# Linear attention and a gated feed-forward layer: first-chunk projection in three float32r products, a new order of work, buffer slots by list, and 32 opening matmuls of ones

## Chip, cores and metric

One core of one Trainium2 chip. The metric is device time in microseconds (us) from one run of the program. The kernel before took 948.82 us (median of three runs, 946.91 to 949.45). All data is float32 in device memory.

## Reference

```python
# q, k, v: (8 batches, 8 heads, 576 positions, 64);  w_a, w_b: (512, 1536);  w_out: (1536, 512)
q_s = softmax(q, over the 64 channels)           # + 1e-9 in the denominator
k_s = softmax(k, over the 576 positions)
kv  = einsum('bhsd,bhse->bhde', k_s, v)
x   = einsum('bhsd,bhde->bhse', q_s, kv)         # -> (4608 tokens, 512)
out = ((x @ w_a) * (x @ w_b)) @ w_out            # -> (4608, 512)
```

## The kernel before, in words

**Chunks.** The 4608 tokens are worked in nine chunks of 512. A chunk needs its attention output x (four pieces of 128 channels by 512 tokens), the two wide products a and b (1536 columns each, in twelve blocks f of 128), their elementwise product g, and the projection of g with `w_out`, summed over the twelve f in four accumulators `po0` to `po3`, one for each 128 tokens.

**Precision.** Most products are made from two-part operands: a float32 value is rounded to float32r (high part, a ScalarE copy, line L202) and the rest is kept as a second float32r value (low part, a VectorE subtraction, L205). A product is then three float32r matmuls: high by high, high by low, low by high. The helper that makes both parts is `split`. `g_split` calls it for g, `split_wo` for a block of `w_out`.

**Chunks 1 to 8** run in six pairs of blocks each. A pair makes seven products in a Strassen manner (`product`, L685, 12 float32r matmuls of 256 columns each), combines them on VectorE and ScalarE into `cc`, splits g (`gh`, `gl`) and projects it (`project`, L706, 12 float32r matmuls of 512 columns for each f).

**Chunk 0** goes block by block, while weights, keys and queries are still coming in. `gate_part` (L660) makes a and b of block f with 24 float32r matmuls of 512 columns. `gate_half` copies a out of PSUM (ScalarE, L667) into a tile `ga` with the tag `gh0` or `gh1`, `gate_end` multiplies it by b (VectorE, L671), and `project_first` (L695) projects the result with plain float32 matmuls: four for each f, one for each 128 tokens. The plain form needs neither `g_split` nor `split_wo`; the splits of the twelve blocks of `w_out` are needed by chunk 1 first.

**Weights** arrive as 64-bit words and are turned into float32 by `float_parts`: two ScalarE passes (L226, L227), a VectorE shift (L230), a GpSimd addition (L233) and a VectorE join (L236). Steps `a.f`, `b.f` and `out.f` are this conversion for the blocks of `w_a`, `w_b` and `w_out`; from f = 4 on the converted block of `w_out` is moved by DMA into its lasting place (`wo_w<-wy`). `sums.i` makes sums of weight blocks on GpSimd for the seven products (L348), `w0.i` to `w6.i` fetch or make the operands, each into one of eight `ws` buffers.

**Order.** Every engine runs its instructions in the order in which they are issued. A table `ORDER` names, for each of five queues (PE is TensorE, DVE is VectorE, Activation is ScalarE, Pool is GpSimd, SP issues the DMAs), the steps in the order wanted: `gate.5*3` takes the next three instructions of that step, `gate.5:6` takes the one that is seventh among those left. What is not in the list comes behind it, in the order of a scheduler that works with the costs of a model. Before, the list of PE ends with the first pair of chunk 2 (`pair.6`).

**Buffers.** A tile pool hands out the buffers of one tag in turn (`ws` 8, `xo` 11, `wy` 8, and so on); a tile waits until the last reader of the tile that had its buffer before is done.

**Start.** The queries (`q_load`), keys (`k_load_t`) and values of chunk 0 come first. `mc`, `ek`: maximum and exponential of the keys; `qs`, `qe`: maximum and exponentials of the queries; `tr` (L969) and `pq` (L1027): transposes on TensorE; `pk`: key-value products (L437); `px` (L604): x; `xh`, `xl`: its two parts; `g00` and so on: `gate_part` of the first blocks.

Of the kernel before, what the change touches and what calls it, by code (L numbers as in the profile page):

```python
# [147 lines left out]
    ),  # L148
}


@with_exitstack
def linear_attention_then_gated_ffn(
# [18 lines left out]
    nc = tc.nc  # L172
# [1199 lines left out]
```

## Time and profile before

| what | value |
|---|---|
| runs, median of three | 948.82 us |
| profiled execution, own time | 951.55 us |
| its span, first to last instruction | 949.7 us |
| TensorE matmuls busy | 928.4 us, 98%, 6479 instructions |
| VectorE busy | 613.7 us, 65% |
| ScalarE busy | 390.5 us, 41% |
| GpSimd busy | 104.8 us, 11% |
| DMA | 282.64 MB, mean 298 GB/s |
| TensorE in the chain that ended last | 89% of the span |

The profiled execution is one run, 2.73 us above the median of the three; 1.85 us of its time lie outside the span. Busy time of TensorE is taken from modelled ends of pipelined matmuls, so the row cannot tell a TensorE at its peak from one that is held up for short times. A plain float32 matmul stands in the trace as two rows, so that the 48 of `project_first` are 96 rows.

### The profile page before, as it was taken

Reading aid. Unit: us, or ns where it says so; the run is one execution under the profiler, and the core shown is the slowest. Engines: PE = TensorE matmul, PEld = TensorE weight load, DVE = VectorE, ACT = ScalarE, POOL = GpSimd, SP = SyncE. Lnnn points to the kernel's source line nnn. Section 1 sums busy time; section 2 is a strip of 40 time slices with the busy share of each in tenths; the row PEclk is TensorE's granted clock in tenths of the full one; section 3 lists DMA queues with packets and bytes.
Section 4 is the critical chain, followed back from the end, with each engine's and each line's share of the span. In section 5 each row is a group of like instructions: output and inputs, shape, how many; then the busy total and the mean of one; then the engine's idle time right before and its main releaser. Section 6 shows DMA issues by size and latency. Waiting matters only on the chain.

```text
span 949.7 us, 17529 instructions
## 1 busy us (share of the span) xinstructions
PE 928.4 (98%) x6479; PEld 825.9 (87%) x6479; DVE 613.7 (65%) x1209; ACT 390.5 (41%) x1085; POOL 104.8 (11%) x88
## 2 busy tenths in 40 slices
PE   5999999999999999999999999999999999999998
PEld 4666668889899999999999999999999999999997
DVE  6978889788685656664757566665756456553443
ACT  7986856424362226222723153334422353121111
POOL 2544452330010001000100000000000000000000
PEclk9999999999999999999999999999999999999999
DMA  9999888899999869896989688976996789577761
GB/s 345 409 389 360 331 315 297 325 330 353 291 380 303 314 255 343 271 353 221 336 273 381 235 283 303 364 273 248 341 334 222 261 284 330 209 262 252 262 214 53
DMA packets 97588, 282.64 MB, mean 298 GB/s; under 512 B 11680, under 2 KB 12256, under 8 KB 97504
## 3 DMA queue, kind: packets, MB, share of 16 engines
q1 hardware_dynamic: 97504, 281.52, 82.7%
q8 instruction: 52, 0.85, 0.3%
q14 instruction: 32, 0.26, 0.1%
HBM read 241.40 MB, written 37.98 MB: 294 GB/s over the span
## 4 chain that ended last, share of the span: by engine, by line
PE 89%; DMA 4%; DVE 4%; SPq 1%; ACT 1%; issue 1%; DVEq 0%; ACTq 0%
PE po L706 27%; PE kp L685 13%; PE ka L685 13%; PE kx L685 13%; PE pt L660 7%; PE ky L685 7%; PE po L695 4%; PE px L616 2%; PE pk L437 2%; DMA ws<-dw 1%; DMA mr<-dq 1%; SPq L571 1%; DMA raw<-in_w_ab 1%; PE px L604 1%; DVE ws L205 1%
## 5 line engine op out<-in xcount | busy, mean ns | idle before, releaser
L706 PE MATMUL po<-wo_w,gh 128*128 128x512 f32 x768 | 227.3, 395 | 0.6 <-ACT gh L202 0.6
L685 PE MATMUL kx<-xo,ws 128*128 128x256 f32 x1152 | 163.1, 283 | 1.3 <-DMA ws<-dw 1.3
L685 PE MATMUL ka<-xo,ws 128*128 128x256 f32 x1152 | 160.8, 282 | 1.1 <-DVE cc L1313 1.1
L706 PEld LDWEIGHTS po<-wo_w,gh 128*128 128x128 f32 x768 | 138.1, 188 | 26.6 <-ACT gh L202 1.1
L685 PE MATMUL kp<-xo,ws 128*128 128x256 f32 x1152 | 158.2, 283 | 0.0
L685 PEld LDWEIGHTS ka<-xo,ws 128*128 128x128 f32 x1152 | 149.5, 188 | 5.5 <-DVE cc L1313 1.3
L685 PEld LDWEIGHTS kx<-xo,ws 128*128 128x128 f32 x1152 | 149.2, 188 | 5.4 <-issue 1.9
L685 PEld LDWEIGHTS kp<-xo,ws 128*128 128x128 f32 x1152 | 148.2, 188 | 4.8 <-issue 0.5
L706 PE MATMUL po<-wo_w,gl 128*128 128x512 f32 x384 | 137.3, 396 | 0.0
L202 ACT CAST gh<-cc 128x512 fp32r<-128x512 f32 x96 | 56.6, 621 | 142.4 <-DVE cc L1309 128.8
L1308 DVE TENSOR_TENSOR cc<-kp,u 128x512 f32<-128x512 f32 x48 | 33.1, 689 | 101.3 <-PE kp L685 101.1
L1296 ACT COPY cc<-kx 128x256 f32<-128x256 f32 x48 | 17.8, 372 | 168.5 <-PE kx L685 168.5
L660 PE MATMUL pt<-xo,ws 128*128 128x512 f32 x288 | 86.7, 441 | 0.0
L706 PEld LDWEIGHTS po<-wo_w,gl 128*128 128x128 f32 x384 | 71.2, 188 | 16.2 <-DVE gl L205 0.7
L530 ACT ACTIVATE qt<-qt,st 128x64 f32<-128x64 f32 x224 | 75.2, 340 | 21.3 <-DVE st L527 18.2
L1295 DVE TENSOR_TENSOR cc<-kp,u 128x512 f32<-128x512 f32 x48 | 33.1, 690 | 76.5 <-PE kp L685 76.2
L685 PE MATMUL ky<-xo,ws 128*128 128x256 f32 x576 | 77.0, 283 | 2.4 <-DMA ws<-dw 0.8
L660 PEld LDWEIGHTS pt<-xo,ws 128*128 128x128 f32 x288 | 53.5, 189 | 24.8 <-issue 13.8
L685 PEld LDWEIGHTS ky<-xo,ws 128*128 128x128 f32 x576 | 71.7, 188 | 3.5 <-DVE xf L802 2.1
L205 DVE TENSOR_TENSOR gl<-cc,gh 128x512 fp32r<-128x512 f32 x96 | 64.0, 685 | 10.7 <-ACT gh L202 10.6
L367 POOL PARTITION_ALL_REDUCE mx<-m x20 | 18.3, 916 | 446.0 <-DVE m L378 446.0
L1277 ACT COPY u<-kx 128x512 f32<-128x512 f32 x48 | 28.0, 584 | 93.8 <-PE kx L685 85.4
(147 smaller groups left out, 1145.1 us busy)
## 6 DMA issues: line engine op xcount, KB each, us to landing
ws<-dw SPq DMA_DIRECT2D x312, 512.0 KB, 5.3
dw<-ws SPq DMA_DIRECT2D x42, 512.0 KB, 6.4
mr<-dq SPq DMA_DIRECT2D x112, 128.0 KB, 4.3
raw<-in_w_ab SPq DMA_DIRECT2D x24, 512.0 KB, 8.3
out<-ot SPq DMA_DIRECT2D x36, 256.0 KB, 4.5
vt<-in_v SPq DMA_DIRECT2D x28, 325.0 KB, 7.1
qt<-in_q SPq DMA_DIRECT2D x32, 256.0 KB, 5.4
kt<-in_k SPq DMA_DIRECT2D x24, 320.0 KB, 5.2
```

The source lines that it names most:

```text
L202: nc.scalar.copy(out=hi, in_=src)
L205: return nc.vector.tensor_tensor(out=lo, in0=src, in1=hi.bitcast(F32), op=ALU.subtract)
L437: nc.tensor.matmul(pk[h * D:(h + 1) * D], kt[:, j, h], vt[:, j, h], start=(j == 0), stop=(j == J - 1),)
L530: nc.scalar.activation(out=qt[:, j, h], in_=qt[:, j, h], func=AF.Exp, bias=st[:, h, 0, j:j + 1], accum_out=st[:, h, 1, j:j + 1],)
L616: nc.tensor.matmul(px[:, s], w, m[:, s], start=(i == 0), stop=(i == 2))
L660: nc.tensor.matmul(pt, w[:, wp], x[g][:, xp], start=(g == 0 and i == 0), stop=(g == NP - 1 and i == 2),)
L685: ins = nc.tensor.matmul(pt[:, n], w[:, n, wp, c], x[:, xp, c], start=(first and n == 0 and i == 0), stop=(i == 5), skip_group_check=True,)
L695: nc.tensor.matmul(po[t], g[:, t * P:(t + 1) * P], wo_first[f], start=(f == 0), stop=(f == NF - 1),)
L706: ins = nc.tensor.matmul(po[t], a[:, ts], wo[f][:, w], start=(f == 0 and i == 0), stop=(f == NF - 1 and i == 2),)
L1277: nc.scalar.copy(out=u2, in_=kx)
L1295: nc.vector.tensor_tensor(out=cc[:, 3], in0=kp, in1=u3, op=ALU.add)
L1308: nc.vector.tensor_tensor(out=cc[:, 1], in0=kp, in1=u2, op=ALU.add)
```

## The change

It has five parts.

1. **Projection of chunk 0.** For f = 0, 1, 2 nothing changes (`PLAIN = 3`). For f = 3 to 11 `project_first` first splits g (`g_split`, one ScalarE copy and one VectorE subtraction) and then calls `project`, that is twelve float32r matmuls instead of four plain ones. `split_wo(f)` is called just ahead of it, no longer in the first pairs of chunk 1. For those f the tile `ga` is one of four parts of a tile with the tag `cc`, so that `gh` and `gl` are free for the two parts.
2. **32 matmuls of ones**, 128 by 128 in plain float32, into the accumulator bank `po3`, ahead of everything else on TensorE. Nobody reads the sums. The matrix of ones is set by GpSimd, as before.
3. **New order.** All five lists are new. The lists of PE and DVE reach to the end of chunk 2 (`pair.11`, `early.11`) instead of its first pair, SP's to the operands of `pair.11`. The first loads stand in the list too: the first queries come ahead of the first keys, and the identity matrix after them.
4. **Slots by list.** The pool is wrapped by a class that gives each tile a named slot with a buffer of its own: first by a list `SLOTS`, then the slot that was given longest ago.
5. **Attention in chunk 2** is no longer pinned behind the last VectorE combination of the pair; its place comes from the list.

```diff
     "PE": (
-        "tr1*4 tr0*5 tr1 pk0*10 pk1*10 pq0*4 tr2*5 pq1*4 px0 tr3:4 tr3*4 pq2*4 pk2*10 pk3*10 px1 "
-        "g00:6 g00:6 g00:6 g00*3 pq3*4 px2 g10:6 g10:6 g10:6 g10:6 g10:6 g10:6 g00*3 g10*3 g00*3 px3 "
...
+        "warm*32 tr0*5 tr1:4 pq0*4 tr1*4 pk0*10 pq1*4 pk1*8 px0 tr2:4 pk1*2 tr2*4 tr3*5 px1 pq3*4 "
+        "pk3*10 pk2*10 pq2*4 g00 g00:5 g00*2 g00:3*2 g00 g00:2 px2 g00 g10:6*2 g00:1 g10*2 g00:1 "
...
     "Activation": (
-        "ek0 qe0 qe0:5 qe0:1 ek1 qe0:3 qe1 qe0:1 qe0 cA1 qe0:1 qe0 cA0 ek2 wc00:1 wc00 qe2 qe2:3 "
...
+        "qe0 qe0:4 qe0:3 qe0 qe0:3 qe0:2 qe0:1 qe1 ek0 qe0 ek1 cA0 wc00*2 qw0 qe2 qe2:2 qe2:1 qe2:2 "
+        "cA1 qe2:2 ek2 qe2:1 qe3 qw1 ek3 qe2:1 qe2 wh00 cA3 cA2 wc10:1 wc10 xh0 wc01:1 wc01 xh1 qw2 "
...
     "SP": (
+        "lq0 lq1 lk1 lk0 eye lw00 lq2 lk2 lq3 lv0 lv1 lk3 lw01 lw10 lv3 lv2 lw11 load.2 lw20 lo0 lw21 "
...
+SLOTS = {
+    "mr": "011",
+    "xo": "0a98765431209a876549a876549a876549a31207",
...
+    "ws": (
+        "076543127065413276054132760541327605431267054312607435126074531260754312607541360257143602"
+        "571436027"
+    ),
...
+    WARM = 32
+    PLAIN = 3
...
+    class Slots:
+
+        def __init__(self, pool, bufs):
+            self.pool, self.bufs, self.past = pool, bufs, {}
+
+        def tile(self, shape, dtype, name, tag=None, bufs=None):
+            tag, bufs = tag or name, bufs or self.bufs
+            past, given = self.past.setdefault(tag, []), SLOTS.get(tag, "")
+            if len(past) < len(given):
+                slot = int(given[len(past)], 36)
+            else:
+                slot = min(range(bufs), key=lambda n: len(past) - past[::-1].index(n) if n in past else n - bufs)
+            past.append(slot)
+            return self.pool.tile(shape, dtype, name=name, tag=f"{tag}.{slot}", bufs=1)
...
+    warm = ps.tile([P, P], F32, name="warm", tag="po3")
+    with named("warm"):
+        for n in range(WARM):
+            nc.tensor.matmul(warm, ones, ones, start=True, stop=True)
...
     def gate_half(f, pt):
-        ga = sb.tile([P, T], F32, name="ga", tag=f"gh{f % 2}", bufs=1)
+        if f < PLAIN:
+            ga = sb.tile([P, T], F32, name="ga", tag=f"gh{f % 2}", bufs=1)
+        else:
+            if f == PLAIN:
+                at["gas"] = sb.tile([P, 4, T], F32, name="ga", tag="cc", bufs=1)
+            ga = at["gas"][:, f % 4]
...
     def project_first(f, g, po):
+        if f >= PLAIN:
+            with named(f"cut.{f}"):
+                parts = g_split(f, g)
+            project(f, parts, po)
+            return
...
+        if f - 1 >= PLAIN:
+            with named(f"split.{f - 1}"):
+                split_wo(f - 1)
         with named(f"proj.{f - 1}"):
             project_first(*pending, po)
...
-                attend(c > 1 and last)
+                attend((c - 1) * NI + i >= 2 * NI and last)
```

More of the change, by code (lines that the diff above doesn't have):

```diff
@@ L172, in linear_attention_then_gated_ffn, with named @@
     nc = tc.nc
+    traced = nc.cur_bb.bb.instructions
+    work = {}
+    @contextmanager
+    def named(name):
+        before = traced[-1] if len(traced) else None
+        yield
+        start = next((n for n in reversed(range(len(traced))) if traced[n] is before), -1) + 1
+        for ins in traced[start:]:
+            work.setdefault((ins.engine, name), []).append(ins)
     B, NP, P, J, _, D = k.shape
@@ L187, in linear_attention_then_gated_ffn @@
     dr = ctx.enter_context(tc.tile_pool(name="dr", bufs=1, space=bass.MemoryType.DRAM))
+    class Slots:
[10 more added lines that the diff above has]
+            return self.pool.tile(shape, dtype, name=name, tag=f"{tag}.{slot}", bufs=1)
+    sb = Slots(sb, 2)
     ident = const.tile([P, P], F32, name="ident")
-    nc.sync.dma_start(out=ident, in_=eye)
+    with named("eye"):
+        nc.sync.dma_start(out=ident, in_=eye)
     ones = const.tile([P, P], F32, name="ones")
     nc.gpsimd.memset(ones, 1.0)
+    warm = ps.tile([P, P], F32, name="warm", tag="po3")
+    with named("warm"):
+        for n in range(WARM):
+            nc.tensor.matmul(warm, ones, ones, start=True, stop=True)
     nc.scalar.preload_act_table(AF.Exp)
@@ L853, in linear_attention_then_gated_ffn @@
     loads = len(nc.cur_bb.bb.instructions)
-    for n in (0, 1):
-        k_load_t(0, n, first[n][0])
-        q_load(0, n, first[n][2])
-    for n in (0, 1):
-        v_load(0, n, first[n][1])
-    for n in (2, 3):
-        k_load_t(0, n, first[n][0])
-        q_load(0, n, first[n][2])
-        v_load(0, n, first[n][1])
-        if n == 2:
-            load_ab(0, 0)
-    for n in ((0, 1), (1, 0), (1, 1)):
-        load_ab(*n)
-    load_o(0)
-    load_ab(2, 0)
-    load_ab(2, 1)
-    load_o(1)
+    for n in range(NP):
+        with named(f"lk{n}"):
+            k_load_t(0, n, first[n][0])
+        with named(f"lq{n}"):
+            q_load(0, n, first[n][2])
+        with named(f"lv{n}"):
+            v_load(0, n, first[n][1])
+    for f in range(3):
+        for n in range(2):
+            with named(f"lw{f}{n}"):
+                load_ab(f, n)
+        if f < 2:
+            with named(f"lo{f}"):
+                load_o(f)
     xfs[1] = sb.tile([P, NP, T], F32, name="xf", bufs=1)
@@ L936, in linear_attention_then_gated_ffn @@
              query_task(2), query_task(3)] + [late_key_task(g) for g in range(1)]
-    load_o(2)
-    tasks[0][0]()
-    load_f(3)
-    tasks[1][0]()
+    with named("lo2"):
+        load_o(2)
+    with named("load.0"):
+        tasks[0][0]()
+    with named("raw.3"):
+        load_f(3)
+    with named("load.1"):
+        tasks[1][0]()
     slow = (0, 1, 0, 1)
@@ L1111, in linear_attention_then_gated_ffn @@
     x0 = [None] * NP
-    traced = nc.cur_bb.bb.instructions
-    work = {}
-    @contextmanager
-    def named(name):
-        before = traced[-1]
-        yield
-        start = next(n for n in reversed(range(len(traced))) if traced[n] is before) + 1
-        for ins in traced[start:]:
-            work.setdefault((ins.engine, name), []).append(ins)
     by_hand = len(traced)
@@ L1167, in arrange @@
                 behind_each_other([chain[-1], ins])
-    behind_each_other([ins for ins in traced[loads:by_hand] if ins.engine == E.SP])
     po = at["po"]
@@ L1225, in run_pending @@
         else:
+            if f >= PLAIN:
+                with named(f"split.{f}"):
+                    split_wo(f)
             project_first(f, ghl, po)
@@ L1237, in part @@
             def part(name):
-                return named(f"{name}.{(c - 1) * NI + i}") if c < 3 else nullcontext()
+                return named(f"{name}.{(c - 1) * NI + i}") if c < 4 else nullcontext()
             def operand(op):
@@ L1271, in linear_attention_then_gated_ffn @@
                     for f in (2 * i + 2, 2 * i + 3):
-                        with named(f"split.{f}"):
-                            split_wo(f)
+                        if f < PLAIN:
+                            with named(f"split.{f}"):
+                                split_wo(f)
             multiply(kx, A11, B11, True)
@@ L1289, in linear_attention_then_gated_ffn @@
             with part("attend"):
-                attend(c > 1 and last)
+                attend((c - 1) * NI + i >= 2 * NI and last)
             kp = ps.tile([P, 2, H], F32, name="kp", tag="k1")
@@ L1304, in linear_attention_then_gated_ffn @@
             with part("attend"):
-                attend(c > 1 and last)
+                attend((c - 1) * NI + i >= 2 * NI and last)
             multiply(kp, S4, B22, False)
```

10 lines of the change are left out of this document (7 added, 3 removed), and 298 rows, old and new, of the table ORDER.

## The prediction

> **What bounds the kernel now.** I read the page first: how much TensorE is busy, and what the chain that ended last is made of.
>
> ```profile
> span 949.7 us, 17529 instructions
> ...
> PE 928.4 (98%) x6479; PEld 825.9 (87%) x6479; DVE 613.7 (65%) x1209; ACT 390.5 (41%) x1085; POOL 104.8 (11%) x88
> ...
> PE 89%; DMA 4%; DVE 4%; SPq 1%; ACT 1%; issue 1%; DVEq 0%; ACTq 0%
> ```
>
> The reader should see a kernel that TensorE bounds nearly everywhere. An average hides stages, so next comes busy time by stretch: the start, the two parts of chunk 0, the handover to chunk 1 with its first pairs, one stretch that overlaps these, and the steady part (length, then busy time of PE, PEld, DVE, ACT, POOL, granted clock, DMA share, GB/s).
>
> ```profile
> 0.00:24.00 24.00, 12.21 (x117) 9.95 (x117) 16.43 (x38) 18.26 (x54) 5.27 (x11) 1.00 0.93 345
> 24.00:60.00 36.00, 35.84 (x155) 24.17 (x154) 30.47 (x58) 33.87 (x84) 17.87 (x13) 1.00 1.03 411
> 60.00:140.00 80.00, 80.00 (x359) 54.26 (x358) 64.84 (x115) 55.90 (x132) 38.08 (x28) 1.00 0.91 336
> 140.00:250.00 110.00, 106.17 (x769) 94.05 (x767) 86.85 (x170) 45.24 (x119) 25.23 (x18) 1.00 0.93 323
> 60.00:160.00 100.00, 99.26 (x490) 69.28 (x489) 82.88 (x146) 68.19 (x168) 46.64 (x33) 1.00 0.91 336
> 250.00:900.00 650.00, 648.20 (x4785) 602.18 (x4786) 396.07 (x799) 230.44 (x687) 18.32 (x20) 1.00 0.82 293
> ```
>
> From 24 to 140 us TensorE never rests, and VectorE is 81% busy beside it (64.84 of 80). The steady part idles 1.8 of 650 us. TensorE work taken out of chunk 0 therefore shortens the run, as long as VectorE, ScalarE and DMA keep up. Room for a better order is left in two places only: the first 24 us (11.8 idle) and 140 to 250.
>
> Third, the chain of waits from 136 to 255 us gives the rate of undisturbed runs of matmuls (start, length, what).
>
> ```profile
> 145.88 1.72 PE po L695 x4
> ...
> 149.01 1.43 PE ka L685 x12
> ...
> 198.20 5.57 PE po L706 x24
> ```
>
> So a plain row of `project_first` costs 1.72/4 = 0.430 us, a float32r matmul of 512 columns 5.57/24 = 0.232, one of 256 columns 1.43/12 = 0.119. The mean durations of the groups (some 0.6, 0.4 and 0.28 us) overlap and cannot be added.
>
> With these rates the idle time of 140 to 250 can be told from its groups:
>
> ```profile
> L706 PE MATMUL po<-wo_w,gh 128*128 128x512 f32 x80 | 24.3, 397 | 0.0
> L685 PE MATMUL kx<-xo,ws 128*128 128x256 f32 x156 | 22.2, 287 | 1.3 <-DMA ws<-dw 1.3
> L685 PE MATMUL ka<-xo,ws 128*128 128x256 f32 x144 | 20.7, 287 | 1.1 <-DVE cc L1313 1.1
> L685 PE MATMUL kp<-xo,ws 128*128 128x256 f32 x144 | 20.3, 288 | 0.0
> L706 PE MATMUL po<-wo_w,gl 128*128 128x512 f32 x40 | 14.4, 400 | 0.0
> L685 PE MATMUL ky<-xo,ws 128*128 128x256 f32 x72 | 9.7, 285 | 0.7 <-DVE ga L671 0.7
> L695 PE MATMUL po<-wo_w,ga 128*128 128x512 f32 x14 | 7.1, 599 | 0.0
> ```
>
> 120 x 0.232 + 516 x 0.119 + 14 x 0.430 = 95.3 us; the small groups left out fill 110 − 3.8 − 95.3 = 10.9 us at most. The idle time is thus 3.8 us by the stretch's row and somewhat more, as modelled ends cover short stalls; I take 7 as its top. Its owners are VectorE (`cc`, `ga`) and a DMA (`ws`).
>
> **The change part by part: the projection.** The rows and the helpers' prices:
>
> ```profile
> L695 PE MATMUL po<-wo_w,ga 128*128 128x512 f32 x64 | 31.6, 595 | 0.0
> ...
> L202 ACT CAST gh<-cc 128x512 fp32r<-128x512 f32 x96 | 56.6, 621 | 142.4 <-DVE cc L1309 128.8 <-PE pm L384 8.0 <-DVE cc L1314 3.4
> ...
> L205 DVE TENSOR_TENSOR gl<-cc,gh 128x512 fp32r<-128x512 f32 x96 | 64.0, 685 | 10.7 <-ACT gh L202 10.6
> ...
> L205 DVE TENSOR_TENSOR ws<-ws_y,ws 128x512 fp32r<-128x512 f32 x24 | 21.4, 898 | 2.3 <-ACT ws L202 2.2
> ```
>
> 64 rows are the eight blocks whose weights lie in `wo_w` at four matmuls and two rows each. One block costs 8 x 0.430 = 3.44 us plain and 12 x 0.232 = 2.78 us in three products: 0.66 us less, for nine blocks **−5.9 us**. TensorE is the limit there, so it all counts, if the feeders hold.
>
> The feeders get more. Nine `g_split` add 9 x 0.685 = 6.2 us to VectorE and 9 x 0.621 = 5.6 us to ScalarE, all before the end of chunk 0's projection. The splits of `w_out` are only moved, but forward:
>
> ```profile
> L205 DVE TENSOR_TENSOR wo_w<-wo_w x8: 677/682/686, 99.4 to 218.0; 128x512 fp32r<-128x512 f32 x8
> ...
> L205 DVE TENSOR_TENSOR wo_w<-wo_w x3: 679/681/686, 99.4 to 125.5; 128x512 fp32r<-128x512 f32 x3
> L205 DVE TENSOR_TENSOR wo_w<-yo,wo_w x2: 685/687/689, 79.5 to 124.9; 128x512 fp32r<-128x512 f32 x2
> ```
>
> Five of the twelve ran by 140 us, the last at 218; now nine must run before their projections, so about four come forward, 4 x 0.68 = 2.7 us. VectorE needs 82.9 + 8.9 = 91.8 us in a stretch (60 to 160) that TensorE leaves in about 100 − 5.9 = 94.1. This is the tightest spot of the change: 2.3 us of air, where 17.1 were. ScalarE has more (68.2 + 5.6 + 2.5 = 76.3). What makes it bearable is that VectorE's work is not bound to this stretch: parts of `sums`, `x.1` and the attention of chunk 2 can slip beyond 160, where VectorE is 79% busy. I cost the new load at nothing, with 0 and +8.9 us as its ends; if the cover is gone it costs what rival two says.
>
> New waits: each projection now waits for a copy on ScalarE and a subtraction on VectorE, 1.3 us behind `gate_end`; TensorE has the 24 matmuls of the next block (5.6 us) to put between. The last of these splits also holds the tile `cc` of pair 0, whose first VectorE write stands behind them in the list anyway: nothing. No DMA is added; the same bytes in a stretch 4% shorter bring its share from 0.93 to about 0.97, under the 1.03 at 411 GB/s that 24 to 60 reaches: nothing.
>
> **The ones.** The matrix is ready early, and the first real matmuls wait for ScalarE:
>
> ```profile
> 0.72 0.21 POOL L192 MEMSET ones<- 128x128 f32 x1 [0.29 <-POOLq L1356]
> ```
>
> ```profile
> 7.96 1.97 PE L969 MATMUL pka<-ident,kt_first 128*128 128x128 f32 x8 [7.96 <-ACT kt_first L963]
> ...
> 12.17 2.44 PE L437 MATMUL pk<-vt_first,kt_first 128*64 128x65 f32 x40 [1.82 <-ACT kt_first L974]
> ...
> 17.60 1.11 PE L969 MATMUL pka<-ident,kt_first 128*128 128x128 f32 x4 [1.94 <-ACT qw L1034]
> 18.50 0.42 PE L969 MATMUL pkb<-ident,kt_first 128*128 128x128 f32 x1
> ...
> 20.95 0.60 PE L969 MATMUL pka<-ident,kt_first 128*128 128x128 f32 x4
> 21.39 0.60 PE L1027 MATMUL pq<-ident,qts 128*128 128x128 f32 x4
> ```
>
> The same four transposes take (18.50 − 17.60)/4 = 0.225 us each at 17.6 and (21.39 − 20.95)/4 = 0.11 at 20.95: TensorE runs at half speed up to about 20 us, though the clock column says 1.00. The 32 matmuls are 64 rows of this length (0.430/4 for a quarter of the columns gives the same 0.11), so they end between 0.9 + 64 x 0.11 = 8.0 us and 0.9 + 64 x 0.225 = 15.3 us. Then TensorE works at full speed: of its 12.2 busy us before 24, most run in half the time. But it waited for ScalarE all that while (1.82, 1.94), and ScalarE, 18.3 of 24 us busy, has no less to do. So little of this shortens the start: at best the 1.8 + 1.9 us that those waits last, at worst the transposes are held from 8 to 15 us and the ScalarE copies behind them, +4 with the queries' exponentials that ScalarE does meanwhile. SP's queue is moved too: queries ahead of keys, the identity behind four loads. Only the transposes need the identity, and ScalarE's first exponentials begin slightly sooner. I take **−0.7 us**, nearer to the good end because the waits are rows and the holding is not.
>
> The Trainium skill (TensorE: Matmul & The Clock Gate, part 1) says that a cold array runs at half its clock and that about 3.4 us of sustained matmuls free it; the two transposes' rates agree. By its figure the ones would take 3.4 us cold and the rest at 0.11, and end near 9.8 us (an estimate).
>
> **The order and the slots.** Bounds: all idle time of 140 to 250 (at most −7) and 1 us elsewhere can go; or new waits of the same size come up, +3, where a planned moment is missed in a list that now fixes all of chunk 2. I take **−2.5 us**, a third of the top: the longer lists aim at this stretch, but VectorE, which owns half of its stalls, has more to do just before.
>
> Sum: −5.9 − 0.7 − 2.5 = −9.1. The profiled execution (951.55 us, 1.85 beside its span) would become 942.4; it was 2.7 us above the median, so on the median 948.8 − 9.1 = **939.7 us**.
>
> **Rivals.** *One: the order finds nearly all of the idle time.* −5.9, −3.7 at the start, −7 in the handover: 932, and 930 with the steady part's 1.8. For it: those stalls have single owners. Against: VectorE's load.
>
> *Two, the other side: VectorE bounds the end of chunk 0.* If its 17.1 idle us from 60 to 160 are waits that no order fills (for GpSimd's additions and ScalarE's copies), the stretch lasts 100 + 8.9 instead of 94.1, and the run 948.8 + 8.9 = 957.7; if half fills, about 950. It is slower than before from the point where more than 2.3 + 5.9 = 8.2 of the 17.1 us stay idle. For it: 81% busy in a queue in strict order. Against: TensorE loses nothing there today.
>
> The rows also show that a subtraction takes 898 ns on `ws_y` against 685 on `cc`. The Trainium skill (SBUF — State Buffer, Who interferes with whom) says that a VectorE instruction with two SBUF inputs and a GpSimd one that reads SBUF lock each other out; the new subtractions are of that kind and fall where GpSimd is busiest. By the two rows that is 9 x 0.21 = 1.9 us more on VectorE, which leaves 0.4 of the 2.3 us: it speaks for this rival, to which I would give 0.10 without it.
>
> *Three: given back.* The 5.9 us go into new waits of the list or into DMA (share 0.93 already): 946 to 951. *Four: the ones do harm*, +4 at the start: 944, still faster.
>
> **How the numbers follow.** Chances: forecast, with four, 0.55 (936 to 944); one 0.18; three 0.14; two 0.13. A measurement tells about 0.3% (2.8 us) from nothing. Faster: 0.55 + 0.18 + 0.03 of three = 0.76; same: 0.11 of three and 0.01 of two; slower 0.12. The range 930 to 950 leaves out most of two and the far end of three and one.
>
> **What would show it.** Right: no L695 rows beyond f = 2 (24 left), 108 more of L706; TensorE without idle time from 24 to 140; transposes at 0.11 from the first; the end of chunk 0 about 6 us sooner; VectorE above 90% there. Wrong: TensorE waiting for `gl`, `ga` or `ws` of VectorE between 60 and 160, or for DMA beyond 160; the first transpose later than 11 us with ScalarE idle ahead of it; more idle time in chunk 2 than the steady part's 1.8 of 650 us would give it.

## The result, and the profile after

The changed kernel takes 953.44 us (median of 15 runs, 951.90 to 959.54) against 948.84 us (15 runs, 946.73 to 954.91) of the kernel before on the same chip: ratio 1.0054, 95% interval 1.0036 to 1.0072. It is 4.6 us slower, where 9.1 us less were forecast. Its profiled execution took 953.44 us, 1.7 of them outside the span; that of before took 951.55.

The page of the changed kernel, first lines of busy time and of the chain that ended last:

```profile
span 951.7 us, 17728 instructions
...
PE 931.0 (98%) x6579; PEld 839.7 (88%) x6579; DVE 611.4 (64%) x1218; ACT 395.8 (42%) x1094; POOL 108.8 (11%) x88
...
PE 82%; DMA 11%; DVE 3%; SPq 2%; issue 1%; ACT 0%; POOL 0%; DVEq 0%; POOLq 0%
```

TensorE looks as busy as before. What moved is the chain: DMA holds 11% of it where it held 4%, and TensorE 82% where it held 89%. The stretches that the prediction used (columns as there), and 250 to 360 us, which it did not look at by itself, for both kernels:

```profile
0.00:24.00 24.00, 20.52 (x193) 17.55 (x194) 17.59 (x47) 19.66 (x57) 4.04 (x11) 1.00 0.92 349
24.00:60.00 36.00, 36.00 (x154) 24.87 (x154) 33.59 (x56) 34.80 (x86) 22.59 (x15) 1.00 0.93 344
60.00:140.00 80.00, 80.00 (x442) 63.92 (x442) 70.37 (x127) 64.06 (x152) 36.77 (x23) 1.00 0.93 329
140.00:250.00 110.00, 101.56 (x716) 92.10 (x715) 79.46 (x167) 44.44 (x122) 27.70 (x20) 0.97 0.92 317
250.00:360.00 110.00, 105.36 (x781) 96.32 (x781) 68.66 (x141) 37.56 (x105) 2.84 (x4) 1.00 0.93 324
```

```profile
250.00:360.00 110.00, 109.83 (x819) 101.87 (x820) 76.75 (x158) 45.25 (x140) 5.28 (x6) 1.00 0.84 307
```

The reader should see three things. From 24 to 140 us TensorE still never rests. From 140 to 250 it idles 8.4 us (3.8 before). From 250 to 360 it idles 4.6 us, where the kernel before (the second fence) idled 0.2.

Two kernels of different pace are compared better by work than by time. The matmuls of the seven products number 84 for a pair and 504 for a chunk; product 0 opens chunk 1, product 504 chunk 2, product 1008 chunk 3. Their starts in the timeline, changed kernel first (start, length):

```profile
131.83 0.28 PE L830 MATMUL ka<-xo,ws 128*128 128x256 f32 x1
...
353.52 1.52 PE L830 MATMUL kx<-xo,ws 128*128 128x256 f32 x12
```

```profile
141.76 1.69 PE L685 MATMUL kx<-xo,ws 128*128 128x256 f32 x12
...
348.68 1.59 PE L685 MATMUL kx<-xo,ws 128*128 128x256 f32 x12
```

Chunk 1 opens 9.9 us earlier. Chunk 3 opens 4.8 us later, so that chunks 1 and 2 take 221.7 us instead of 206.9. The stretches between these points (length, TensorE busy, clock, DMA share, GB/s), first the changed kernel, then the kernel before, each with the rest of the run:

```profile
131.83:353.52 221.69, 208.61 (x1518) 0.98 0.92 317
353.52:948.00 594.48, 594.07 (x4347) 1.00 0.79 281
```

```profile
141.76:348.68 206.92, 202.92 (x1504) 1.00 0.89 317
348.68:946.00 597.32, 595.65 (x4347) 1.00 0.78 277
```

So the books close: −9.9 up to chunk 1, +14.8 in chunks 1 and 2, −2.8 in the rest, +2.0 in all, which is 951.7 − 949.7. (The medians differ by 4.6 because the profiled execution of before lay 2.7 above its median.)

Two of these three numbers need care. Product 0 is not the end of chunk 0, whose projection runs on among the first products: 25 of its 108 float32r rows in the changed kernel (5.8 us at 0.232 each), 12 of its 96 plain rows before (5.2 us at 0.430). So 0.6 us of the 9.9 only moved behind product 0. And the −2.8 can't be put down to the change: by the counts of matmul rows the rest is the same work in every kernel of this document, and it took 594.5 to 601.4 us in their traces, 594.9 to 599.0 in those with the old order.

Of the +14.8, 9.1 are idle time (13.08 against 4.00). The clock of 0.98 is another 3.4 us, told under the hardware below. Of the last 2.3, 0.6 is the work that moved; the others I take for short stalls that modelled ends cover.

What TensorE waited for in that stretch of the changed kernel (us in total, times, longest):

```profile
PE kx L830 <- DMA ws<-dw: 6.2, 4, 2.2
PE ka L830 <- DMA ws<-dw: 2.7, 2, 1.4
PE kp L830 <- DVE m L518: 1.5, 1, 1.5
PE px L756 <- ACT qh L342: 1.4, 1, 1.4
```

Before, the same view has one wait of 1.3 us on the loads of operands into `ws`; now there are six, 8.9 us together. SP, which issues these loads, has a new wait of its own. Its longest entry from 100 to 345 us, for the changed kernel and then for the kernel before:

```profile
SPq L471 <- DMA dw<-ws: 38.5, 13, 5.7
```

```profile
SPq L327 <- DVE ws L205: 29.8, 16, 4.5
```

Before, SP mostly waited for VectorE to finish an operand that it was to store. Now it waits for the store that must have left a buffer before the next operand is loaded into it. Whether this wait is what TensorE pays for is tested below (slots dealt anew); it is not.

### The profile page after: what moved, and what is told of

Read it like the earlier page. It is cut to its first block, busy times and chain, and to the rows that moved or that the text cites. A ratio compares the mean times of both kernels' runs of the same rounds, so it can differ in the third digit from the quotient of the medians.

```text
span 951.7 us, 17728 instructions
## 1 busy us (share of the span) xinstructions
PE 931.0 (98%) x6579; PEld 839.7 (88%) x6579; DVE 611.4 (64%) x1218; ACT 395.8 (42%) x1094; POOL 108.8 (11%) x88
## 4 chain that ended last, share of the span: by engine, by line
PE 82%; DMA 11%; DVE 3%; SPq 2%; issue 1%; ACT 0%; POOL 0%; DVEq 0%; POOLq 0%
PE po L856 26%; PE kp L830 12%; PE kx L830 12%; PE ka L830 12%; PE pt L800 6%; PE ky L830 6%; DMA ws<-dw 4%; DMA dw<-ws 3%; PE pk L577 2%; PE px L756 2%; DMA mr<-dq 1%; PE po L845 1%; SPq L711 1%; PE warm L332 1%; DMA dq<-sst 1%
## 5 line engine op out<-in xcount | busy, mean ns | idle before, releaser
L856 PE MATMUL po<-wo_w,gh 128*128 128x512 f32 x840 | 262.5, 396 | 0.0
L830 PE MATMUL kx<-xo,ws 128*128 128x256 f32 x1152 | 184.3, 284 | 6.7 <-DMA ws<-dw 6.2
L830 PE MATMUL ka<-xo,ws 128*128 128x256 f32 x1152 | 182.0, 283 | 3.6 <-DMA ws<-dw 3.1
L830 PE MATMUL kp<-xo,ws 128*128 128x256 f32 x1152 | 172.6, 283 | 1.8 <-DVE m L518 1.5
L856 PEld LDWEIGHTS po<-wo_w,gh 128*128 128x128 f32 x840 | 151.3, 188 | 25.7 <-issue 0.4
L830 PEld LDWEIGHTS kx<-xo,ws 128*128 128x128 f32 x1152 | 160.7, 190 | 12.7 <-DVE ws L345 2.5
L830 PEld LDWEIGHTS ka<-xo,ws 128*128 128x128 f32 x1152 | 159.7, 189 | 9.9 <-issue 1.6
L856 PE MATMUL po<-wo_w,gl 128*128 128x512 f32 x420 | 152.9, 397 | 0.0
L856 PEld LDWEIGHTS po<-wo_w,gl 128*128 128x128 f32 x420 | 78.0, 189 | 15.0 <-DVE gl L345 0.4
L830 PE MATMUL ky<-xo,ws 128*128 128x256 f32 x576 | 87.8, 283 | 0.0
```

The lines of the kernel that those rows point to most:

```text
L830: ins = nc.tensor.matmul(pt[:, n], w[:, n, wp, c], x[:, xp, c], start=(first and n == 0 and i == 0), stop=(i == 5), skip_group_check=True,)
L856: ins = nc.tensor.matmul(po[t], a[:, ts], wo[f][:, w], start=(f == 0 and i == 0), stop=(f == NF - 1 and i == 2),)
```

## The experiments

All kernels below were timed against the kernel before, on the same chip for each group. The milestones are from one profiled execution of each, and executions differ: that of order alone lies 5.5 us above its median, that of no ones 5.0 us below. A difference of a few us between two milestones is therefore told from nothing only where several kernels agree.

| kernel | median, us | ratio (95%) | product 0 | 504 | 1008 | end of last |
|---|---|---|---|---|---|---|
| before | 948.84 | 1 | 141.8 | 246.9 | 348.7 | 946.0 |
| changed | 953.44 | 1.0054 (1.0036 to 1.0072) | 131.8 | 244.9 | 353.5 | 948.0 |
| products alone | 962.99 | 1.0136 (1.0115 to 1.0157) | 150.8 | 259.6 | 360.4 | 958.7 |
| order alone | 965.10 | 1.0168 (1.0129 to 1.0206) | 140.0 | 257.2 | 363.8 | 965.2 |
| ones alone | 951.46 | 1.0022 (1.0006 to 1.0038) | 142.1 | 248.5 | 349.4 | 948.4 |
| no ones | 957.46 | 1.0071 (1.0048 to 1.0093) | 131.6 | 242.0 | 349.7 | 947.0 |

### One part at a time

**Ones alone**, in the kernel before, and **no ones**, in the changed one.

```diff
+    opening = [nc.tensor.matmul(warm, ones, ones, start=True, stop=True).ins for n in range(32)]
...
-        "tr1*4 tr0*5 tr1 pk0*10 ...
+        "warm*32 tr1*4 tr0*5 tr1 pk0*10 ...
```

> The kernel before with the 32 matmuls of ones in front and nothing else. If cold matmuls hold the start up: first gate matmul 1 to 2 us sooner than 23.9 us, 946.5 to 948. Rival (ScalarE sets the start, and the transposes now begin at 10 us instead of 8): 948 to 951.

```diff
-    WARM = 32
+    WARM = 0
```

> The changed kernel without its 32 matmuls of ones. If the ones make the start faster and this reaches the end: 2 us slower than the changed kernel, 954 to 957, with the first gate matmul at 23 to 24 us instead of 21.8. Rival (the stalls of chunk 1 swallow what the start brings, as their ends are set by the queue of SP and its stores): 952 to 954, the same as the changed kernel.

Alone the ones gain nothing: they cost 0.2% (interval 0.1 to 0.4%). In the new order it is not settled. Without them the changed kernel measured 957.46 us, as if they were worth some us, but its eleven runs spread from 951.79 to 960.74, the interval of its ratio overlaps that of the changed kernel, and in the profile its first product comes 0.2 us sooner. The start shows no gain from them, in three timelines: changed kernel, without ones, and ones in the old order (start, length, idle time ahead and its releaser).

```profile
0.98 8.95 PE L332 MATMUL warm<-ones 128*128 128x128 f32 x64 [0.98 <-POOL ones L328]
9.76 0.60 PE L1120 MATMUL pka<-ident,kt_first 128*128 128x128 f32 x4
...
21.83 2.15 PE L800 MATMUL pt<-xo,ws 128*128 128x512 f32 x8
```

```profile
8.47 1.12 PE L1120 MATMUL pka<-ident,kt_first 128*128 128x128 f32 x4 [8.47 <-ACT kt_first L1114]
...
21.62 2.16 PE L800 MATMUL pt<-xo,ws 128*128 128x512 f32 x8
```

```profile
17.38 0.66 PE L971 MATMUL pka<-ident,kt_first 128*128 128x128 f32 x4 [2.69 <-ACT qw L1036]
...
24.31 1.97 PE L662 MATMUL pt<-xo,ws 128*128 128x512 f32 x6
```

The transposes do run at the full rate from the first (9.76: four in 0.44 us, by the next row's start of 10.20). But with the old order a faster TensorE only waits longer for ScalarE (2.69 us, where 1.94 stood before), and the first gate block starts at 24.3 us (23.9 before). In the new order it starts at 21.8 with the ones and 21.6 without. The 2.1 us at the start come from the new lists (which of the five, no run shows), not from the ones, which even hold the first transposes back by 1.3 us.

**Products alone**: the old lists, with the twelve-matmul projections of f = 3 to 11, their cuts and the splits of `w_out` put at the earliest places where their inputs are there.

```diff
     def project_first(f, g, po):
+        if f >= PLAIN:
+            with named(f"cut.{f}"):
+                parts = g_split(f, g)
+            with named(f"first.{f}"):
+                project(f, parts, po)
+            return
```

> The kernel before, its order and its buffers, with the nine projections of f = 3 to 11 in three float32r products each; the splits stand where the old order has just finished gate_end of the same f. Theory S (the products are worth what the rates say, and the loss comes from the lists): 942 to 945, first product of chunk 1 some 5 to 6 us sooner than 141.8. Rival F (the splits overload VectorE and ScalarE at the end of chunk 0): 948 to 955, TensorE idle for gl, ga or gh between 60 and 160 us.

It is 14 us slower than before, beyond both ranges expected, and chunk 1 opens 9.0 us late. Stretch 60 to 160 us (columns as above), and TensorE's waits from 24 to 160 us:

```profile
60.00:160.00 100.00, 89.76 (x442) 68.64 (x441) 83.88 (x139) 69.39 (x165) 43.73 (x31) 0.97 0.83 304
```

```profile
PE kx L691 <- ACT ga L673: 3.6, 1, 3.6
PE pt L661 <- DVE ga L677: 1.7, 3, 1.0
PE po L718 <- DVE gl L206: 1.1, 1, 1.1
...
PE po L718 <- DVE wo_w L206: 1.0, 2, 0.8
```

This is rival two of the prediction, in the old order with the splits where I put them: TensorE waits for `ga`, `gl` and `wo_w`, and VectorE does hardly more work in the stretch (83.88 us) than before (82.88), because it waits in its list too (6.2 us for GpSimd's `wr`, 4.1 us for ScalarE's `wo_w`). With these places the cheaper products don't pay; other places in the old order were not tried.

**Order alone**: the new lists, slots and ones, with all projections plain (`PLAIN = 12`, the tile `ga` still in the `cc` slot; the entries for cuts and splits taken out, those of `proj` thinned to four).

```diff
-    PLAIN = 3
+    PLAIN = 12
```

> The changed kernel's order, slots and ones, but the first projection of all twelve f in plain float32, as before: each f takes 4 plain matmuls where its 12 products stood first (f = 10 and 11 at once, ahead of the rest of the first pair), and the splits of w_out go back to the end of chunk 0 and to chunk 1. The other half of the change without the products. The products' own price in chunk 0 by the prediction is 5.9 us, so product 0 should start 5 to 7 us later than with them, 137 to 139 us (131.8 with them). If the stalls of chunks 1 and 2 come from the lists (Theory O), they stay, and the time is 956 to 961 us: the order alone loses 8 to 12 us against the kernel before, and the products win 6 of them back. If the stalls come from the products' lead (Theory E, which the late start already spoke against), 949 to 953 us.

It is 16 us slower than before, some 4 us more than the range expected if the lists are at fault. Its chunk 1 opens at 140.0 us, so the three-product form opens it 8.2 us sooner in the new order. Chunks 1 and 2 take 223.8 us (in an execution 5.5 us above its median): as long as in the changed kernel. With the same lists the waits are alike, too:

```profile
PE kx L821 <- DMA ws<-dw: 7.7, 5, 2.7
PE ka L821 <- DMA ws<-dw: 2.0, 2, 1.3
```

The loss in chunks 1 and 2 belongs to the new order and slots and not to the products. Nor is it the price of coming early, since here chunk 1 comes only 1.8 us earlier than before. All the traces bear this out: from product 0 to 1008 the four kernels with the old lists for TensorE, VectorE and ScalarE (before, ones alone, products alone, and small stores in the kernel before, below) took 206.9 to 209.6 us. Ten with the new lists (changed, no ones, order alone, and those below up to the third SP list, without the two that sort SP's list from its start) took 217.2 to 227.3.

**Late start**: the changed kernel with 27 matmuls of ones (54 rows of 0.11 us, 5.9 us) ahead of chunk 1. Had the work merely run ahead of its loads, the loads would have caught up meanwhile.

```diff
+        "gate.11*4 junk*27 pair.0:24 proj.9 attend.0*10 proj.10:6 proj.10:8 pair.0*4 pair.0:20 proj.10:3 "
...
+                    for n in range(27):
+                        nc.tensor.matmul(junk, ones, ones, start=True, stop=True)
```

> The changed kernel with 27 matmuls of ones (0.22 us each, 5.9 us) put on TensorE right before chunk 1's first product, all else as it is. Theory E (lead eaten: chunks 1 and 2 can't run further ahead of the DMAs, so what TensorE is early there it waits later): most of the 5.9 us is absorbed by shorter stalls, product 0 at 137.7 us, but product 1008 at 353.5 to 355.5, and 953.5 to 955.5 us in all. Theory L (the lists stall TensorE by fixed amounts, whenever it starts): nothing is absorbed, product 1008 at 359 to 360, 959 to 960 us.

962.05 us (ratio 1.0141, 1.0102 to 1.0181), 8.6 above the changed kernel: nothing was absorbed. A lead over the inputs that is simply eaten up does not fit this. The test has a limit: a load that waits for a buffer which TensorE frees is delayed with TensorE, so only the other loads could have caught up.

### Which part of the order: slots, stores, SP's list

**Slots dealt anew**: entries 25 to 99 of the list of `ws` slots.

```diff
-        "076543127065413276054132760541327605431267054312607435126074531260754312607541360257143602"
+        "076543127065413276054132073061457432560240163510423754671205135467024715306274310564732150"
```

> The changed kernel with one edit: of its slot list for ws, entries 25 to 99 (the operands of chunks 1 and 2) are dealt anew, so that a load gets the slot that has been free longest and not one whose own store is still under way. Orders, ones and products stay. Theory S (the slot list makes SP's queue wait 5 to 7 us at a time for a store, and the products behind starve): the 38 us of SP's waits for stores between 100 and 345 us fall below 15, TensorE's stalls between 140 and 345 us fall from some 22 us to 10 to 14, no half-speed stretch of the clock, 941 to 946 us. Rival O (the new order of loads is late whatever the slots): 951 to 955, same stalls in the same places.

952.66 us, ratio 1.003 (1.0013 to 1.0047): 0.8 us better than the changed kernel by the medians, with overlapping intervals. SP's wait for stores, 38.5 us in the changed kernel, is nearly gone:

```profile
SPq L471 <- DMA dw<-ws: 4.2, 3, 2.9
```

TensorE's waits on the loads stay (8.2 and 2.1 us). So neither these slots nor the store that a load must wait for is the main cause.

**Small stores**: the 24 stores of chunk 1's operands are cut to 64 KB each; 10.5 MB fewer are written, and the later loads read another operand's data, of the same size. The same edit in the kernel before is its control, and one kernel has it together with the new slots.

```diff
+    def put_small(i, op, w):
+        few = dr.tile([P, P], F32R, name=f"dw{i}{op}")
+        nc.sync.dma_start(out=few.bitcast(F32), in_=w[:, 0, 0, 0].bitcast(F32))
+        dw[i, op] = dw[i, A11]
...
-                    put_w(i, op, w)
+                    put_small(i, op, w)
```

> The changed kernel, but the 24 stores of chunk 1's operands (512 KB each) write an eighth (64 KB), and chunks 2 on load another operand of the same size in their place; every wait, slot and order stays, 10.5 MB fewer go over the DMA engines between 135 and 330 us, and chunks 2 to 8 are computed from other weights. Theory D: DMA bandwidth is what chunk 1 lacks, TensorE's idle time of 140 to 350 us falls by 8 us or more, and the time is 941 to 947 us. Theory L or O: waits for order, not bytes, hold TensorE, and the time stays within 2 us of the changed kernel's, 951 to 955 us.

> The kernel before with the same 24 smaller stores, as the control: its TensorE idles under 6 us between 140 and 350 us, so Theory D expects at most 2 us of gain, 946.5 to 949.5 us; the difference of the two with smaller stores is then the lead of chunk 0, 3 to 8 us in favour of the changed one. If small stores gain the kernel before 5 us or more, bytes are dear in both, and the comparison says nothing about the change.

> The changed kernel with both edits: the buffers of the weights dealt anew and the 24 stores of chunk 1's operands cut to an eighth (chunks 2 to 8 computed from other weights). Alone the first gave 0.8 us and the second 3.8. If what is left is DMA time (Theory E), the two together free the loads of both holds and give more than their sum: 943 to 947 us, TensorE's waits for loads of weights between 140 and 350 us under 3 us (8.9 in the changed kernel). Theory L: their sum at most, 948 to 950 us.

The changed kernel gains 3.8 us (949.63, ratio 1.0002, 0.9984 to 1.002), the control none (950.82, 1.0016, 1.0000 to 1.0032), slots and small stores together give 951.23 (1.0031, 1.0007 to 1.0054). The DMA load from 140 to 200 us falls from 303 to 239 GB/s, and yet TensorE still waits 4.2 and 1.7 us for operands. So bytes count in the changed kernel by itself, but not on top of the new slots (1.0030 without small stores, 1.0031 with them, where a gain beyond both was expected). How large a part they are stays open.

**SP's list anew**: all of it, or its first 90 DMAs, sorted by when each transfer's reader needs it.

```diff
     "SP": (
-        "lq0 lq1 lk1 lk0 eye lw00 lq2 lk2 lq3 lv0 lv1 lk3 lw01 ...
+        "lq0 lq1 lk0 lk1 eye lw00 lq2 lv0 lk2 lq3 lv1 lk3 lw10 ...
```

> The changed kernel with the list of SP alone written anew (288 DMAs: of those whose data or buffer the trace of the changed kernel shows ready, the one needed first goes first; the other lists, the slots and the ones stay). Theory D (supply): the new list of SP puts stores that wait for VectorE in front of loads that could go, so that by 100 us 3.6 MB fewer have landed than before (34.2 against 37.8 MB), and TensorE's lead of 10 us is lost in chunks 1 and 2 to operands that land late. Then this kernel has 38 MB landed by 100 us, TensorE's idle time between 140 and 350 us falls from 20 us by at least 8, product 1008 starts at 341 to 346 us (353.5 in the changed kernel, 348.7 before), and the time is 941 to 947 us. Theory L (the lists of the computing engines themselves stall TensorE, whatever the DMAs do): the time stays at 951 to 955 us, and product 1008 at 351 to 355.

> As the kernel with SP's list anew, but only its first 90 DMAs (issued up to 105 us in the changed kernel) are put in the new order; from there on SP's list is the changed kernel's. Theory D in its narrow form (what was lost in chunk 0 is what is missing later): 37 to 38 MB by 100 us, and most of the gain of the whole list, 943 to 949 us. Rival O (what costs is the order in chunks 1 and 2, where SP stands before a buffer of the attention with loads of weights behind it): no gain here, 951 to 954 us, and the gain only with the whole list. Theory L: neither gains.

Both are far slower: 980.96 us (1.0337, 1.0306 to 1.0368) and 963.48 (1.0141, 1.0109 to 1.0173). In the second TensorE waits between 60 and 140 us, where it never had to:

```profile
PE po L856 <- ACT wo_w L342: 5.0, 1, 5.0
```

The sort starved the projection of its split `w_out`, and so could not show whether SP's early order is at fault.

**SP's list late**: the new slots, and SP's list sorted anew from its 101st DMA (about chunk 1) only.

```diff
-        "out.9 raw.11 b.8 load.8 a.9 b.6 raw.11*2 attend.0 b.10 b.9 a.10 b.7 sums.0 sums.0:2 sums.0:1 "
...
+        "out.9 raw.11 b.8 load.8 a.9 b.6 raw.11*2 attend.0 b.10 a.10 b.7 b.9 sums.0:1 out.10 load.8 "
...
```

> The kernel with the buffers dealt anew, and SP's list in a new order from its 101st DMA on (chunks 1 and 2): again what is needed first goes first, but nothing goes that would make a more urgent one late at 345 GB/s. Theory O (SP stands before a buffer of the attention, 9.8 us at 180 us in the kernel with new buffers alone, with loads of weights behind it): product 1008 at 344 to 349 us, 943 to 949 us in all. Theory E: DMA time itself lacks, at most 2 us better than with the buffers alone, 950.5 to 953 us. Worse than 954 us: the new order delays a load of the attention, and its chain becomes the bound, as with the whole list anew.

952.85 us (1.0038, 1.0022 to 1.0054): no gain in time, but TensorE waits for other things. Its waits from product 0 to 1008, and one of VectorE from 200 to 250 us:

```profile
PE kp L830 <- DVE u L1422: 3.2, 3, 1.4
PE kp L830 <- DVE cc L1439: 3.0, 1, 3.0
PE px L756 <- ACT qh L342: 2.4, 1, 2.4
PE ka L830 <- DMA ws<-dw: 1.6, 1, 1.6
```

```profile
DVE qtt L717 <- DMA mr<-dq: 3.4, 1, 3.4
```

The waits on operands fall from 8.9 to 1.6 us in this trace. That SP's order with the slots does this is likely and not more: the two repeats of this list below have 8.1 and 6.0 us of them, and the kernel without ones, which keeps the changed kernel's SP list and slots, 5.4. From product 0 to 420, the opening of chunk 1's last pair, it needs 87.9 us (before 87.9, changed 91.2). That the loss up to there was SP's order is not shown by this, as the kernel without ones took 87.6 us in its trace. Nor do old and new lists hold the same work there. By the counts of matmul rows and the rates of the prediction (an estimate), the changed lists have 2.3 us less of it from product 0 to 420, 1.3 more from 420 to 504 and 1.6 more from 504 to 1008. Between products 420 and 504 this kernel then needs 26.6 us against 17.3 before, 9.3 more; TensorE waits there for VectorE, and VectorE for the loads of chunk 2's attention.

**SP's list a third time**: from 190 or 215 us on, so that those loads come 2 to 3 us earlier.

```diff
-        "w6.3 attend.1 attend.6 w5.2 w1.3 w0.4 sums.4 attend.1 w3.3 sums.4:1 ...
+        "w6.3 attend.1 attend.6 w5.2 w1.3 w0.4 sums.4 w3.3 sums.4:1 attend.1:1 ...
```

> The kernel with the buffers dealt anew and SP's late list anew, and that list written once more from its own trace from 190 us on, with the loads of the attention's factors and queries (mr, qtt) pulled 3 us forward. In the trace of the first version TensorE ran from product 0 to product 420 in 88.0 us (87.8 before, 91.3 changed) and then lost 8.3 us between 220 and 250 us, behind VectorE and ScalarE that waited for mr. Theory O (the loss is SP's order in chunks 1 and 2): the loss of 220 to 250 us falls by 3 us or more, product 1008 at 341 to 346 us, 941 to 947 us, under the kernel before. Rival V (there the computing lists themselves, not a load, hold TensorE): product 1008 stays at 348 to 351, 950 to 954 us.

> The same, but rewritten only from 215 us on and with 2 us instead of 3 for mr and qtt, so that the stretch that ran without loss stays untouched to the last DMA. Theory O: 942 to 948 us, and product 420 at 220 us again. Rival V: 950 to 954 us.

957.34 us (1.0075, 1.0051 to 1.0099) and 954.38 (1.0041, 1.002 to 1.0063): not better than the list that they start from. This way of moving these loads forward does not repair the kernel.

### The old lists behind a seam

Here the changed kernel's lists run up to a time T, and the old lists (with their times moved forward, and `ws` in turn or, once, by the changed kernel's slots) behind it: T at the end of chunk 0 (twice), at 200 us and at 222 us. The last two start from the kernel with the late SP list.

```diff
     "PE": (
...
-        "gate.11*4 pair.0:24 proj.9 attend.0*10 proj.10:6 proj.10:8 pair.0*4 pair.0:20 proj.10:3 "
+        "gate.11*4 pair.0 proj.9 pair.0*9 proj.10:6 pair.0*2 proj.10:8 proj.10:3 pair.0*12 proj.10*3 "
...
-                attend((c - 1) * NI + i >= 2 * NI and last)
+                attend(c > 1 and last)
```

> The changed kernel's lists for chunk 0, its products and its ones, and from chunk 1 on the kernel before's order on every engine (the order of its trace, moved 10 us forward, and its shorter lists), its turn-by-turn buffers for the weights and its later pins of the attention. Theory O (the loss of 14.7 us sits in the new lists for chunks 1 and 2): from product 0 to product 1008 it takes 207 to 210 us, as before (206.9; 221.7 in the changed kernel), and the time is 939 to 943 us, better than both. Rival Z (any list loses there when TensorE comes 10 us sooner, as VectorE's, ScalarE's and the DMAs' work of chunk 0 isn't done sooner): 215 us or more, 947 to 953 us.

> The same, but with the changed kernel's list of buffers for the weights kept to its end (100 entries). If the buffers' list is a part of the loss (a load put into a buffer whose own store is under way), this takes 2 to 6 us longer than with turn-by-turn buffers, 942 to 948 us; if the buffers cost nothing, the two agree within 1.5 us.

> The kernel with the new slots and the late SP list up to 200 us (where its products have about the same wait-free pace as the kernel before: product 420 at 220.0 us), and from there on the lists of the kernel before, its times taken 9.1 us earlier, with weight buffers turn by turn. Theory L (the lists of the changed kernel for chunk 2 cost the time behind product 420; the old lists have no stall there, 119.1 us from product 420 to product 1008 against 129.2): product 1008 at about 339 us, total 938 to 943. Theory S (a smaller lead of the inputs over the products costs it, whatever the list): 128 us or more from product 420 to 1008, total 950 or above. A seam that costs again, as at 100 us: TensorE idle over 8 us between 180 and 240 us and product 420 later than 226 us, total above 953.

> The same seam 22 us later, at 222 us, behind product 420, with the attention of chunk 2 wholly by the old lists. Theory L: product 420 at 220 us as with the late SP list, product 1008 at about 339 us, total 938 to 943. Theory S: product 1008 at 348 us or later, total 950 or above. If both seams give about 119 us from product 420 to 1008 the lists of chunk 2 are the cause; if only the earlier one does, what goes wrong in the new lists lies between 200 and 222 us.

| T | median, us | ratio (95%) | product 0 to 420 | 420 to 504 | 504 to 1008 |
|---|---|---|---|---|---|
| no seam: before | 948.84 | 1 | 87.9 | 17.3 | 101.8 |
| no seam: changed | 953.44 | 1.0054 | 91.2 | 21.9 | 108.6 |
| no seam: SP late | 952.85 | 1.0038 | 87.9 | 26.6 | 102.6 |
| end of chunk 0 | 982.57 | 1.0337 (1.031 to 1.0364) | 114.1 | 17.2 | 100.8 |
| the same, the changed kernel's slots | 982.14 | 1.0343 (1.0315 to 1.0371) | 116.5 | 17.2 | 102.8 |
| 200 us | 952.90 | 1.0035 (1.0018 to 1.0052) | 98.0 | 17.3 | 102.0 |
| 222 us | 956.76 | 1.0071 (1.0047 to 1.0095) | 89.8 | 29.2 | 102.5 |

The seam at the end of chunk 0 costs twice. Chunk 1 opens at 150.0 us (147.6 with the changed kernel's slots), 18 us later than in the changed kernel, and from there to product 420 TensorE takes 26 us more than before (114.1 against 87.9). The longest single wait lies ahead of product 0: TensorE waits for VectorE, and VectorE stands before a load of queries (first line: TensorE's waits from 100 to 264 us; second: VectorE's from 100 to 140 us):

```profile
PE pmx L445 <- DVE m L439: 9.2, 1, 9.2
DVE st L578 <- DMA qt<-in_q: 10.6, 1, 10.6
```

Behind product 0 many waits share the loss, the longest 4.3 us. From product 420 on the old lists run without a stall, 118.0 us busy of 118.0, and those behind the seam at 200 us idle 0.6 of 119.2 (first and second fence; columns as for the stretches above):

```profile
264.10:382.10 118.00, 118.00 (x882) 1.00 0.89 312
```

```profile
230.80:350.00 119.20, 118.58 (x881) 1.00 0.89 318
```

From product 420 to 1008 before needed 119.1 us, the changed kernel 130.4. So the new lists of chunk 2 cost time that the old ones do not, from product 504 on: 108.6 us, 1.6 of it more work, against 100.8 to 102.8 with the old lists. SP's late list has 102.6 there too, its two repeats 107.2 and 108.3. But in none of the seams did the old lists keep the lead: each late seam took 10 to 12 us more where it lay, some 2.9 of it work that the seam moved there (an estimate as above). At 200 us it was 10.1 us ahead of product 420 (98.0 against 87.9), at 222 us 11.9 behind it (29.2 against 17.3). In both VectorE stood waiting for loads of chunk 2's attention; its longest entries from 200 to 260 us, for 200 and then 222:

```profile
DVE qtt L647 <- DMA qtt<-in_q_late: 8.1, 2, 6.3
```

```profile
DVE qtt L655 <- DMA mr<-dq: 7.0, 1, 7.0
```

**What stays open.** Five lists (SP late, its two repeats, both late seams) open chunk 2 at 243 to 251 us although they open chunk 1 9 to 10 us before the old kernel, which opens chunk 2 at 246.9. In the three whose waits are shown, VectorE waits for the loads of the coming attention (queries, and the factors `mr`) between 200 and 260 us, as it does at the seam at the end of chunk 0 for that of chunk 1; that this wait is the cause was argued and not tested by itself. Shown is where the loss lies (chunks 1 and 2 under the new lists, with or without the new products and the lead); which wait in them has to go is not. What would deliver these loads in time without starving the operands was not found, and no version measured beats the kernel before.

## Why the prediction was wrong

**The projection (−5.9): right, as far as TensorE's own time goes.** TensorE's groups from 24 to 140 us in the changed kernel:

```profile
L856 PE MATMUL po<-wo_w,gh 128*128 128x512 f32 x66 | 23.3, 404 | 0.0
L845 PE MATMUL po<-yo,ga 128*128 128x512 f32 x24 | 12.2, 592 | 0.0
L856 PE MATMUL po<-wo_w,gl 128*128 128x512 f32 x30 | 11.6, 404 | 0.0
```

The 24 plain rows are there, 96 float32r matmuls have come by 140 us and 12 follow. Chunk 1 opened 9.9 us sooner. By the rates of the prediction, 6.5 of this are cheaper rows ahead of product 0 (84 plain rows before; 24 plain and 83 float32r rows now): the forecast 5.9 and the 0.6 that moved behind it. Another 2.1 came at the start; the last 1.3 I can't assign. Order alone opens chunk 1 1.8 us sooner only because four more plain rows (1.7 us) stand behind product 0; what it wins at the start (1.8 us) it idles away from 60 to 140 us (2.2 us). The cover named for VectorE held: it was 88% busy from 60 to 140 (70.37 of 80), just short of the 90 that I named, and TensorE waited for nothing there. *Rival two* fell for this order and came true for the old one as I arranged it, at 14 us instead of 8.9. The surcharge that the prediction put on the subtractions, 0.21 us each from another row's mean, was mostly not there: of eight into `gl` from 60 to 140 us (shortest, median and longest in ns), seven took the plain price and one double.

```profile
L345 DVE TENSOR_TENSOR gl<-ga,gh x8: 676/679/1527, 61.9 to 136.1; 128x512 fp32r<-128x512 f32 x8
```

The long one began at 99.23 us, while a GpSimd addition ran from 98.47 to 100.21. The Trainium skill (SBUF — State Buffer, Who interferes with whom) says that a VectorE instruction with two SBUF inputs contends with a GpSimd one that reads SBUF; this one row agrees, and nothing hung on it.

**The ones and the start (−0.7): right in sign, wrong in source.** The first gate block came 2.1 us sooner, inside the bounds; it does so without the ones too, so it came from the lists and not from a faster TensorE, and that it fell on the side of the forecast is luck. *Rival four* (the ones hold the first transposes) is true in kind, 1.3 us instead of 4, with 0.2% for the ones alone.

**The order and the slots (−2.5, at worst +3): this step failed.** Chunks 1 and 2 took 14.8 us more, 14.1 without the work that moved there, and order alone loses as much without the products. Two things were wrong in its working. I bounded it by the idle time of 140 to 250 us, but the lists of PE and DVE fix work up to the end of chunk 2, about 350 us. The row of 250 to 360 before has 0.17 us idle: there a new list can only lose, and it lost 4.5 us of idle time. And I took new waits of the size of the old ones, +3, for the worst case. A new list can bring many new waits: six loads of operands came too late for TensorE, by up to 2.2 us each (8.9 together, 1.3 before), with waits for VectorE and ScalarE besides, and the half clock behind two of them added 3.4 us for which the sum had no term. Why these loads come late stays open. The store that must first leave a buffer is not the reason, as the slots dealt anew show (4.2 us of SP's waits instead of 38.5, and no less waiting of TensorE); fewer bytes or another SP list shifted the waits, and no run removed the loss.

**Rival three (given back into new waits of the list or into DMA, 946 to 951)** had the mechanism and the place, though not the size: the result lies 2.4 us beyond it, as it let at most the 5.9 us won be lost and a little more. At 0.14 it was given too little. *Rival one* fell: the stalls it would have removed more than doubled.

The signs listed under "wrong" were the right ones: TensorE waiting for DMA beyond 160 us, and more idle time in chunk 2.

## What to carry to other kernels

Time a new order by itself, apart from the cheaper work that comes with it: here the order alone cost 1.7%, and the cheaper products won back only a part. A new order for a stretch without idle time can only lose there, so the idle time that it could remove says nothing of what it can cost. Compare kernels by the start of the same piece of work, not by time windows: that told the 9.9 us won from the 14.8 lost. Then count which other work stands on either side of that point, and look at the same stretch in every kernel that shares the lists, since one trace alone can be some us off.

## What the hardware showed

TensorE's clock can fall after gaps of about 2 us. In the changed kernel waits of 1.95 and 2.18 us (timeline rows) were each followed by a stretch at half clock (windows: length, busy, clock, DMA share, GB/s):

```profile
149.68 0.35 PE L830 MATMUL kx<-xo,ws 128*128 128x256 f32 x1 [1.95 <-DMA ws<-dw]
...
170.22 0.71 PE L830 MATMUL kx<-xo,ws 128*128 128x256 f32 x4 [2.18 <-DMA ws<-dw]
```

```profile
151.00:154.40 3.40, 2.91 (x12) 0.50 0.73 258
154.40:171.50 17.10, 14.92 (x104) 1.00 0.96 308
171.50:174.90 3.40, 3.40 (x17) 0.50 0.64 146
```

Two stretches of 3.4 us at half rate cost about 3.4 us, nearly as much as the waits ahead of them (4.1 us). The kernel before has none between 20 and 948 us. So a stall of 2 us in this TensorE-bound kernel can cost nearly twice its length. It does not always: the clock stayed at 1.00 behind a gap of 2.60 us in the kernel without ones (at 234 us) and one of 2.19 us in that with the seam at 222 us (at 146 us). The Trainium skill (TensorE: Matmul & The Clock Gate, part 1) lets the clock drop after an idle window of about 3.4 us; here single gaps of about 2 us were enough in these two places, and the measurement decides.
